# Moving the Gelu slope into the attention phase, and prefetching the gradient stage, in a fused transformer-block backward kernel

## The chip, the cores and the metric

The kernel runs on one core of one Trainium2 chip. The metric is the device time of one execution in microseconds. PE is the matmul engine, DVE the vector engine, ACT the activation engine, POOL the GpSimd engine, SP the engine that issues most transfers; 16 DMA engines move the data.

## The reference, cut to what matters

The program computes one block and all its gradients: `x + attention(xn) * silu(mlp(xn))`, S = 2048 rows, D = 512, 32 heads of 16, MLP width F = 1792, everything in bf16.

```python
x = A_x
xn = _layernorm(x)
s = _A_ref(xn, A_wqkv, A_wo)                 # softmax attention, 32 heads of 16
y = _layernorm(xn)
h = _gelu(y @ B_w1 + B_b1)                   # tanh form of Gelu
g = _silu(h @ B_w2 + B_b2)
out = x + s * g
# outputs: out, and the gradients of x, wqkv, wo, w1, b1, w2, b2 (jax.vjp)
```

The Gelu slope, gelu'(h1) with h1 = y·w1 + b1, is an F × S array (7.3 MB in bf16). It multiplies the incoming gradient in the MLP backward.

## The kernel before

It has three parts: a forward pre-stage (layer norms, qkv, MLP forward; it stores h1 in DRAM as `H1T_s`), attention forward and backward in one software-pipelined loop of 1024 steps, and a gradient stage for everything else.

One attention step, in program order (PE products `s`, `t`, `d`, exp on ACT, the product `gts` on DVE, then transposes by DMA from the SP queue):

```python
etp = sb("etp", 3); gtp = sb("gtp", 4); gbp = sb("gbp", 5); ekp = sb("ekp", 5)
...
for hj in range(2):    # emit_mult: one of these per head of the pair
    nc.vector.tensor_tensor(out=gts[:, kb % 2, hj, :]..., in0=ds[hj][:]..., in1=st_et[g][:, :, kb % 4, hj, :], op=ALU.mult)
# emit_dmat: every second step 512 KB of gts, every fourth step 512 KB of et, are transposed SBUF to SBUF
nc.sync.dma_start_transpose(out=blk[j]["Gk"][kc][:, h], in_=st_gt[g][:]...)          # gk <- gts
nc.sync.dma_start_transpose(out=ek[:]..., in_=st_et[g][:, 2:4]...)                   # ek <- et
```

The gradient stage computes the slope from h1 on ACT and DVE, in 28 groups of 1024 columns:

```python
def emit_gp(sc):                      # called four times, spread over the stage
    for f0, nf in FG:                 # 7 groups
        nc.scalar.dma_start(out=h1[:], in_=k.H1T_s[...])
        nc.scalar.activation(out=x2t[:], in_=h1[:], func=ACT.Square)
        ...                           # 7 DVE operations, 2 Sigmoids
```

Its order: output projection with `transpose_to` on PE for O and dm (`ps_so`), dwo, dw2, MLP gradient (`ps_dhg`, `ps_dy`), then one block of loads (wqkvT, dQT, R, xn, dQn, dKVn), dx and dwqkv (`ps_dxa`, `ps_dwq`), and dw1 (last group `ps_dw`).

Of the kernel before, what the change touches and what calls it, by code (L numbers as in the profile page):

```python
# [16 lines left out]
NT = S // 128  # L17
# [255 lines left out]
def phase3(ctx, tc, k, A_x, A_wqkv, A_wo, B_w1, B_w2, grad_out, out_0, out_1, out_2, out_3, out_4, out_5, out_6, out_7, dbg):  # L273
# [5 lines left out]
    GA = 0.044715  # L279
    GC = float(np.sqrt(2.0 / np.pi))  # L280
    FG = [(0, 2), (2, 2), (4, 2), (6, 2), (8, 2), (10, 2), (12, 2)]
    with ExitStack() as c1:
        big = c1.enter_context(tc.tile_pool(name="p3_big", bufs=1))
        psA = c1.enter_context(tc.tile_pool(name="p3_psA", bufs=5, space=PSUM))
        psT = c1.enter_context(tc.tile_pool(name="p3_psT", bufs=2, space=PSUM))
        psS = c1.enter_context(tc.tile_pool(name="p3_psS", bufs=1, space=PSUM))
        dxm_all = big.tile([128, NT, D], bf16, name="dxm_all")
        ones_bf = big.tile([128, 1], bf16, name="ones_bf")
        nc.vector.memset(ones_bf[:], 1.0)

        with ExitStack() as cAB:
            bAB = cAB.enter_context(tc.tile_pool(name="p3ab_big", bufs=1))
            gpp = cAB.enter_context(tc.tile_pool(name="p3_gp", bufs=3))
            gwk = cAB.enter_context(tc.tile_pool(name="p3_gwk", bufs=2))
            dmT = bAB.tile([128, IC, S], bf16, name="dmT")
            w2T = bAB.tile([128, IC, F], bf16, name="w2T")
            w1T = bAB.tile([128, FC, D], bf16, name="w1T")
            gps = {}
            dh_state = {}

            def emit_gp(sc):
                gp = gpp.tile([128, FC, 512], bf16, name="gp")
                gps[sc] = gp
                for f0, nf in FG:
                    h1 = gwk.tile([128, nf, 512], bf16, name="g_h1")
                    nc.scalar.dma_start(out=h1[:], in_=k.H1T_s[f0 * 128:(f0 + nf) * 128, sc * 512:(sc + 1) * 512].rearrange("(c p) s -> p c s", p=128))
                    x2t = gwk.tile([128, nf, 512], bf16, name="g_x2")
                    nc.scalar.activation(out=x2t[:], in_=h1[:], func=ACT.Square)
                    v = gwk.tile([128, nf, 512], bf16, name="g_v")
                    nc.vector.tensor_scalar(out=v[:], in0=x2t[:], scalar1=GA, scalar2=1.0, op0=ALU.mult, op1=ALU.add)  # L310
                    nc.vector.tensor_tensor(out=v[:], in0=v[:], in1=h1[:], op=ALU.mult)
                    sg = gwk.tile([128, nf, 512], bf16, name="g_sg")
                    nc.scalar.activation(out=sg[:], in_=v[:], func=ACT.Sigmoid, scale=2.0 * GC)
                    nc.vector.tensor_scalar(out=x2t[:], in0=x2t[:], scalar1=6.0 * GA * GC, scalar2=2.0 * GC, op0=ALU.mult, op1=ALU.add)
                    nc.vector.tensor_tensor(out=x2t[:], in0=x2t[:], in1=h1[:], op=ALU.mult)
                    nc.scalar.activation(out=v[:], in_=v[:], func=ACT.Sigmoid, scale=-2.0 * GC)
                    nc.vector.tensor_tensor(out=v[:], in0=v[:], in1=sg[:], op=ALU.mult)
                    nc.vector.tensor_tensor(out=v[:], in0=v[:], in1=x2t[:], op=ALU.mult)
                    nc.vector.tensor_tensor(out=gp[:, f0:f0 + nf, :], in0=v[:], in1=sg[:], op=ALU.add)

            with ExitStack() as c2:
                b2 = c2.enter_context(tc.tile_pool(name="p3a_big", bufs=1))
                wk = c2.enter_context(tc.tile_pool(name="p3a_wk", bufs=3))
                hgp = c2.enter_context(tc.tile_pool(name="p3a_hg", bufs=2))
                dm_all = b2.tile([128, NT, D], bf16, name="dm_all")
                otp = c2.enter_context(tc.tile_pool(name="p3a_ot", bufs=2))
                wo_sb = b2.tile([128, IC, D], bf16, name="wo_sb3")
                nc.sync.dma_start(out=wo_sb[:], in_=A_wo.rearrange("(c p) b -> p c b", p=128))
                hgcs = {}

                def load_hg(i):
                    hgcs[i] = hgp.tile([128, NT, 256], bf16, name="hgc")
                    nc.sync.dma_start_transpose(out=hgcs[i][:], in_=k.HGT_s[i * 256:(i + 1) * 256, :])
                psdb2 = psS.tile([1, D], f32, name="psdb2")
                for t in range(NT):
                    oT = otp.tile([128, IC, 128], bf16, name="oT")
                    transpose_to(nc, psT, oT, k.Oall[:, t, :], k.ident_bf, IC, 0, t)
                    ps = psA.tile([128, D], f32, name="ps_so", tag="mm")
                    for cc in range(IC):
                        nc.tensor.matmul(ps[:], lhsT=oT[:, cc, :], rhs=wo_sb[:, cc, :],  # L340
                                         start=(cc == 0), stop=(cc == IC - 1))
                    gb = wk.tile([128, 2, D], bf16, name="gb3")
                    (nc.sync if t % 2 == 0 else nc.scalar).dma_start(out=gb[:], in_=k.GB_s[t * 128:(t + 1) * 128, :, :])
                    xt = wk.tile([128, D], bf16, name="xt3")
                    (nc.scalar if t % 2 == 0 else nc.sync).dma_start(out=xt[:], in_=x2[t * 128:(t + 1) * 128, :])
                    nc.vector.tensor_tensor(out=dm_all[:, t, :], in0=ps[:], in1=gb[:, 1, :], op=ALU.mult)
                    t1 = wk.tile([128, D], f32, name="t13")
                    nc.vector.tensor_tensor(out=t1[:], in0=ps[:], in1=gb[:, 0, :], op=ALU.mult)
                    ot = wk.tile([128, D], bf16, name="ot3")
                    nc.gpsimd.tensor_tensor(out=ot[:], in0=t1[:], in1=xt[:], op=ALU.add)  # L350
                    nc.sync.dma_start(out=o0[t * 128:(t + 1) * 128, :], in_=ot[:])
                    transpose_to(nc, psT, dmT, dm_all[:, t, :], k.ident_bf, IC, t, 1)
                    nc.tensor.matmul(psdb2[0:1, :], lhsT=ones_bf[:, 0:1], rhs=dm_all[:, t, :], start=(t == 0), stop=(t == NT - 1))
                    if t == 1:
                        load_hg(0)
                    if t == 2:
                        load_hg(1)
                    if t == 3:
                        nc.sync.dma_start_transpose(out=w2T[:], in_=B_w2)
                        nc.sync.dma_start_transpose(out=w1T[:], in_=B_w1)  # L360
                db2 = wk.tile([1, D], bf16, name="db2")
                nc.vector.tensor_copy(out=db2[:], in_=psdb2[:])
                nc.sync.dma_start(out=out_7.rearrange("(o d) -> o d", o=1), in_=db2[:])
                emit_gp(0)
                dwo_ps = [psA.tile([128, D], f32, name="ps_dwo", tag="mm") for _ in range(IC)]
                for t4 in range(4):
                    dso = otp.tile([128, 4, D], bf16, name="dso3")
                    nc.scalar.dma_start(out=dso[:], in_=k.DSO_s[t4 * 512:(t4 + 1) * 512, :].rearrange("(t p) d -> p t d", p=128))
                    for ac in range(IC):
                        for tt in range(4):  # L370
                            t = t4 * 4 + tt
                            nc.tensor.matmul(dwo_ps[ac][:], lhsT=k.Oall[:, t, ac * 128:(ac + 1) * 128], rhs=dso[:, tt, :],
                                             start=(t == 0), stop=(t == NT - 1))
                for ac in range(IC):
                    dwo = otp.tile([128, D], bf16, name="dw_out")
                    nc.scalar.copy(out=dwo[:], in_=dwo_ps[ac][:])
                    nc.sync.dma_start(out=out_3[ac * 128:(ac + 1) * 128, :], in_=dwo[:])
                emit_gp(1)
                for i in range(7):
                    for fl in range(2):  # L380
                        fc = 2 * i + fl
                        ps = psA.tile([128, D], f32, name="ps_dw2", tag="mm")
                        for t in range(NT):
                            nc.tensor.matmul(ps[:], lhsT=hgcs[i][:, t, fl * 128:(fl + 1) * 128], rhs=dm_all[:, t, :], start=(t == 0), stop=(t == NT - 1))  # L384
                        dw2 = otp.tile([128, D], bf16, name="dw_out")
                        nc.scalar.copy(out=dw2[:], in_=ps[:])
                        nc.sync.dma_start(out=out_6[fc * 128:(fc + 1) * 128, :], in_=dw2[:])
                    if i + 2 < 7:
                        load_hg(i + 2)
# [526 lines left out]
```

## Time and profile before

The median is 2693.51 us in 3 runs (2687.11 to 2696.66); the profiled execution spans 2682.9 us.

| stretch, us of the span | length | what |
|---|---|---|
| 0–272 | 272 | pre-stage |
| 272–2191 | 1919 | attention |
| 2191–2683 | 492 | gradient stage |

Windows of the kernel before (start and end, length, then busy us of PE, its weight loads, DVE, ACT, POOL; granted PE clock; DMA share; GB/s). The DMA share adds up the times of all packets over the time of 16 engines, so it exceeds 1 where packets overlap. The rows are attention, projection, dw2, the block of loads, and dw1.

```profile
272.00:2191.00 1919.00, 1768.16 (x15620) 480.01 (x15620) 1548.33 (x2624) 1470.54 (x1537) 273.18 (x708) 0.99 1.15 228
2191.00:2291.00 100.00, 54.49 (x199) 18.43 (x200) 76.18 (x124) 52.85 (x62) 21.65 (x16) 0.51 0.77 195
2309.00:2364.00 55.00, 49.71 (x222) 21.64 (x220) 32.04 (x56) 33.20 (x41) 0.00 (x0) 0.97 0.87 180
2470.00:2526.00 56.00, 1.66 (x8) 0.58 (x6) 3.40 (x10) 2.20 (x4) 0.00 (x0) 0.56 1.06 259
2624.00:2683.00 59.00, 50.95 (x447) 44.00 (x445) 6.53 (x15) 5.22 (x14) 0.00 (x0) 0.97 0.56 123
```

In the projection PE runs at half clock with a chain of short dependences; in the 56 us hole PE does nothing. The hole, in the timeline of the SP queue (start, duration, line, what is issued):

```profile
2488.92 24.95 SPq L433 DMA_TRANSPOSE wqkvT<-in_A_wqkv_dram  x1
2513.92 9.72 SPq L434 DMA_TRANSPOSE dQT<-dQ_s  x1
2523.69 21.99 SPq L438 DMA_TRANSPOSE dKVn<-dKVT_s  x1
```

Last, gts, the DVE product on the chain of waits: its 2048 instances (min/median/max ns), and, from the view of waits in attention, how long DVE stood before it for a gts buffer that a gk transpose still held (us in total, times, longest).

```profile
L640 DVE TENSOR_TENSOR gts<-d,et x2048: 669/681/694, 286.5 to 2169.2; 128x512 bf16<-128x512 f32 x187
...
DVE gts L640 <- DMA gk<-gts: 0.8, 1, 0.8
```

### The profile page before, as it was taken

The page shows a single profiled execution, that of the slowest core. Times are in us where ns is not written, and L with a number is a line of the kernel's source. Part 1 is how long each engine was busy: PE and PEld are TensorE (multiplying, and loading weights), DVE is VectorE, ACT ScalarE, POOL GpSimd, SP SyncE. Part 2 cuts the span into 40 slices and gives each one's busy share as a digit, 9 for nine tenths or more (in the row PEclk, how much of TensorE's full clock was granted, in tenths as well). Part 3 has the DMA queues.
Part 4 walks back from the last instruction along what each step waited for, and adds up shares of the span by engine and source line. Part 5 has one row for each costly group of instructions (what it writes and reads, how often), then busy time and mean ns, then how long its engine had stood idle before and what let it go on. Part 6 is the DMA issues. An engine that isn't in the chain of part 4 may idle for free.

```text
span 2682.9 us, 47705 instructions
## 1 busy us (share of the span) xinstructions
PE 2317.8 (86%) x18320; PEld 743.1 (28%) x18320; DVE 1960.5 (73%) x3502; ACT 1733.7 (65%) x1951; POOL 404.5 (15%) x831
## 2 busy tenths in 40 slices
PE   3788799999999999999999999999999965888298
PEld 2333122222222222222222222222222212333147
DVE  5755688888888888888888888888888858775141
ACT  3344577777777777777777777777777755632020
POOL 0433202011110201111011111101111112000020
PEclk8899899999999999999999999999999975899699
DMA  5355999999999999999999999999999997634925
GB/s 188 94 183 179 190 243 225 227 235 230 229 230 237 222 233 227 228 232 232 232 222 236 227 233 232 227 234 225 231 229 235 217 216 187 157 93 97 309 70 116
DMA packets 1877879, 555.92 MB, mean 207 GB/s; under 512 B 1793553, under 2 KB 1861266, under 8 KB 1877650
## 3 DMA queue, kind: packets, MB, share of 16 engines
q1 hardware_dynamic: 1823874, 501.09, 91.9%
q10 hardware_dynamic: 53776, 51.78, 6.2%
q8 instruction: 143, 2.34, 0.4%
q14 instruction: 86, 0.70, 0.1%
HBM read 49.68 MB, written 57.41 MB: 40 GB/s over the span
## 4 chain that ended last, share of the span: by engine, by line
PE 37%; DVE 37%; issue 14%; DMA 7%; POOL 2%; ACT 1%; SPq 1%; ACTq 0%; DVEq 0%; POOLq 0%
DVE gts L640 29%; PE d L605 6%; PE X L686 6%; PE Z L755 4%; PE Z L749 3%; PE t L577 2%; DVE xs L692 2%; DVE xt L704 2%; PE ps_dhg L405 2%; PE ps_dwq L446 2%; PE XT L702 1%; PE X L671 1%; PE ps_h L212 1%; PE ps_dw L474 1%; PE ps_dw L384 1%
## 5 line engine op out<-in xcount | busy, mean ns | idle before, releaser
L640 DVE TENSOR_TENSOR gts<-d,et 128x512 bf16<-128x512 f32 x2048 | 1301.8, 682 | 324.2 <-issue 289.3
L619 ACT ACTIVATE et<-s 128x1024 bf16<-128x1024 f32 x1024 | 997.1, 1023 | 7.9 <-PE d L605 6.5
L627 ACT ACTIVATE e<-t 128x1024 bf16<-128x1024 f32 x512 | 524.3, 1024 | 424.9 <-PE t L577 421.3
L605 PE MATMUL d<-QDT,KVT 32*128 32x512 bf16 x2048 | 595.3, 378 | 117.7 <-DVE gts L640 116.5
L591 PE MATMUL s<-QDT,KVT 32*128 32x512 bf16 x2048 | 398.4, 386 | 14.8 <-DMA QDT<-QDPad 12.7
L671 PE MATMUL X<-et,Lc 128*32 128x512 bf16 x2048 | 398.0, 385 | 14.3 <-DVE xs L692 14.3
L674 PE MATMUL X<-et,NAT 128*32 128x512 bf16 x2048 | 399.1, 387 | 0.0
L686 PE MATMUL X<-gts,NAT 128*17 128x512 bf16 x2048 | 397.6, 384 | 0.0
L755 PE MATMUL Z<-gk,W 128*32 128x512 bf16 x2048 | 395.9, 380 | 0.0
L686 PEld LDWEIGHTS <-NAT 128*17 128x17 bf16 x2048 | 92.4, 87 | 492.1 <-issue 492.1
L719 POOL TENSOR_TENSOR W<-NATQd,rL 128x128 bf16<-128x128 bf16 x64 | 25.8, 403 | 1331.6 <-DVE rL L714 1331.6
L749 PE MATMUL Z<-e,W 128*32 128x512 bf16 x1024 | 201.0, 386 | 3.8 <-DVE acc L762 2.3
L749 PE MATMUL Z<-ek,W 128*32 128x512 bf16 x1024 | 201.8, 390 | 0.0
L577 PE MATMUL t<-KVT,QDT 32*128 32x512 bf16 x1024 | 199.5, 386 | 0.0
L591 PEld LDWEIGHTS <-KVT 32*128 32x128 bf16 x2048 | 96.6, 91 | 351.1 <-issue 351.1
L605 PEld LDWEIGHTS <-KVT 32*128 32x128 bf16 x2048 | 140.3, 90 | 69.2 <-issue 37.6
L671 PEld LDWEIGHTS <-Lc 128*32 128x32 bf16 x2048 | 103.6, 92 | 179.7 <-issue 179.7
L762 DVE TENSOR_TENSOR acc<-Z,acc 64x512 f32<-64x512 f32 x192 | 129.2, 673 | 13.3 <-PE Z L755 13.3
L749 PEld LDWEIGHTS <-W 128*32 128x32 bf16 x2048 | 120.9, 93 | 57.8 <-issue 51.3
L674 PEld LDWEIGHTS <-NAT 128*32 128x32 bf16 x2048 | 100.5, 95 | 50.6
L755 PEld LDWEIGHTS <-W 128*32 128x32 bf16 x2048 | 103.7, 95 | 8.2 <-issue 0.3
L577 PEld LDWEIGHTS <-QDT 32*128 32x128 bf16 x1024 | 48.2, 91 | 202.3 <-issue 202.3
(167 smaller groups left out, 2212.8 us busy)
## 6 DMA issues: line engine op xcount, KB each, us to landing
gk<-gts SPq DMA_TRANSPOSE x512, 4.2
HGT_s<-hgT SPq DMA_DIRECT2D x2, 3584.0 KB, 12.3
g_h<-H1T_s ACTq DMA_DIRECT2D x28, 256.0 KB, 3.3
DH1T_s<-dh1T SPq DMA_DIRECT2D x4, 1792.0 KB, 7.5
NAT<-NAT_s SPq DMA_DIRECT2D x16, 264.0 KB, 3.2
GB_s<-gB ACTq DMA_DIRECT2D x16, 256.0 KB, 2.0
ek<-et SPq DMA_TRANSPOSE x256, 4.1
dKVT_s<-ob SPq DMA_DIRECT2D x64, 64.0 KB, 2.2
```

The source lines that it names most:

```text
L577: nc.tensor.matmul(t[:, hj, :], lhsT=op["QDT"][r:r + 32, q0:q0 + 128], rhs=op["KVT"][r:r + 32, kc * 512:(kc + 1) * 512], start=True, stop= ...
L591: nc.tensor.matmul(s[:, hj, :], lhsT=op["KVT"][r:r + 32, kb * 128:(kb + 1) * 128], rhs=op["QDT"][r:r + 32, qc * 512:(qc + 1) * 512], start ...
L605: nc.tensor.matmul(d[:], lhsT=op["KVT"][r:r + 32, kb * 128:(kb + 1) * 128], rhs=op["QDT"][r:r + 32, qc * 512:(qc + 1) * 512], start=True, ...
L619: nc.scalar.activation(out=et[:, :, kb % 4, :, :].rearrange("k b h q -> k h b q"), in_=st_s.pop(g)[:].rearrange("k h (b q) -> k h b q", b= ...
L627: nc.scalar.activation(out=e[:], in_=st_t.pop(g)[:], func=ACT.Exp)
L640: nc.vector.tensor_tensor(out=gts[:, kb % 2, hj, :].rearrange("k (b q) -> k b q", b=4), in0=ds[hj][:].rearrange("k (b q) -> k b q", b=4), ...
L671: nc.tensor.matmul(X[64 + 32 * hj:96 + 32 * hj, :], lhsT=Lc[:], rhs=et[:, :, kb % 4, hj, :], start=(kb == 0), stop=False, skip_group_check ...
L674: nc.tensor.matmul(X[32 * hj:32 * hj + 32, :], lhsT=NATt[:, kb, hj, 1:33], rhs=et[:, :, kb % 4, hj, :], start=(kb == 0), stop=(kb == 15), ...
L686: nc.tensor.matmul(X[64 + 32 * hj:64 + 32 * hj + 17, :], lhsT=NATt[:, kb, hj, 0:17], rhs=gts[:, kb % 2, hj, :], start=False, stop=(kb == 1 ...
L749: nc.tensor.matmul(Z[32 * hj:32 * hj + 32, :], lhsT=blk[j]["W1"][:, qb, hj, :], rhs=ev[:, hj], start=(qb == qb_order[0]), stop=False, tile ...
L755: nc.tensor.matmul(Z[32 * hj:32 * hj + 32, :], lhsT=blk[j]["W2"][:, qb, hj, :], rhs=gv[:, :, :, hj, qb, :], start=False, stop=(qb == qb_or ...
L762: nc.vector.tensor_tensor(out=av, in0=Z[0:64, :], in1=av, op=ALU.add)
```

## The change

Its intent: the slope is made on POOL during attention, where POOL is idle 86% of the time, a tile of 128 × 512 at a time, one POOL operation per attention step; the result goes to DRAM (`GP_s`) and the gradient stage only loads it. That frees DVE, ACT and SBUF in the gradient stage, which is rewritten: PE transposes become DMA transposes, operands are loaded early into slots shared by tag, dwq is interleaved with the projection and dkv follows it, gradients are computed one group ahead.

The core of the diff (long parts cut):

```diff
 # attention: a generator that is advanced by one operation per step
+    def gelu_slope_ops():
+        def load(i):
+            x = bgp.tile([128, 512], bf16, name="bg_x")
+            nc.sync.dma_start(out=x[:], in_=H1T_s[fc * 128:(fc + 1) * 128, sc * 512:(sc + 1) * 512])
+        for i in range(4 * FC):                       # 56 tiles
+            tt(m, x, x);  yield
+            ts(v, m, GA, 1.0);  yield
+            tt(v, v, x);  yield
+            nc.scalar.activation(out=t[:], in_=v[:], func=ACT.Tanh, scale=GC)
+            ts(m, m, 1.5 * GA * GC, 0.5 * GC);  yield
+            tt(m, m, x);  nx = load(i + 1);  yield
+            ...                                       # five more POOL operations
+            nc.sync.dma_start(out=GP_s[fc * 128:(fc + 1) * 128, sc * 512:(sc + 1) * 512], in_=m[:])
+            yield
...
             emit_finalize((g - 17) // 16)
+        elif g % 16 not in (2, 3):
+            next(bg, None)
 # gradient stage
-            def emit_gp(sc):                          # slope on ACT and DVE: gone
+        def load_gp(i):
+            gps[i] = ring.tile([128, 7, 512], bf16, name="gp", bufs=3)
+            nc.scalar.dma_start(out=gps[i][:], in_=k.GP_s[...])
...
-                    transpose_to(nc, psT, oT, k.Oall[:, t, :], k.ident_bf, IC, 0, t)
+                nc.sync.dma_start_transpose(out=oT[i][:]..., in_=k.Oall[:, 4 * i:4 * i + 4, :]...)
...
+                for ic in range(IC):                  # dwq beside the projection
+                    nc.tensor.matmul(acc4[ic][:], lhsT=xn_all[:, t, ic * 128:(ic + 1) * 128], rhs=k.dQall[:, t, :], ...)
...
-            nc.sync.dma_start_transpose(out=wT[:], in_=A_wqkv)
-            nc.sync.dma_start_transpose(out=dQT[:], in_=k.dQ_s)
-            nc.sync.dma_start_transpose(out=dKVn[:], in_=k.dKVT_s)
+            do_D(3)
+            load_hg(k.DH1T_s, 0)
+            wT = big.tile([128, 12, D], bf16, name="wqkvT", tag="s14a")
+            nc.sync.dma_start_transpose(out=wT[:], in_=A_wqkv)
```

## The prediction

> **What bounds the kernel now.** The stage windows split the 2682.9 us span into: forward pre-stage 0–272, attention 272–2191 (1919 us), gradient stage 2191–2683 (492 us). In attention PE is busy 1768, DVE 1548, ACT 1471, POOL 273 us; the chain of waits alternates between the DVE product gts (29% of the span), PE matmuls and PE issue. No engine has room for more, except POOL. In the gradient stage PE is busy only 365 of 492 us. Its matmuls are about 1440 of 512 columns (the dw1 ones counted as halves); at the 0.216 us each that the dhg run shows (56 in 12.1 us) that is 311 us, so 181 us are waits, a cold clock, and transposes on PE. The windows say where: output projection 2191–2291, 100 us at a granted clock of 0.5, for a cadence of 5 us per row tile in its quiet half; operand loads 2470–2526, 56 us with PE idle (the queue view shows the issues of wqkvT 25, dQT 9.7 and dKVn 22 us in a row on SP); dw2 55 us and dw1 59 us against 48 us of matmuls each, waiting for 1 MB transposes that land in 7–8.5 us.
>
> **What the change does.**
> 1. Removes from the gradient stage the slope chain: 28 groups of about 4.3 us of DVE (119 us) and 3.1 us of ACT.
> 2. PE transposes of O and dm become DMA transposes, so the projection loses its PE–copy–PE round trip; dwqkv (192 matmuls, 41 us) moves there.
> 3. Operands are loaded ahead: the 56 us hole should nearly vanish.
> 4. Adds to attention 56 × (nine or ten POOL operations, one Tanh, two 128 KB transfers).
>
> **Costing the attention part.** Like POOL operations take 0.65–1.5 us (q 0.82–1.23, ot 1.45), about 10 us per tile, 560 us in all; POOL goes from 273 to about 830 of 1919 us and stays off the chain. The Trainium skill's page "SBUF — State Buffer", section "Who interferes with whom", says that a DVE instruction with at most one SBUF input outside the two-port modes does not contend with GpSimd. gts, acc, xs and xt are such, and the trace agrees so far: gts takes 669 to 694 ns in all 2048 cases, POOL running or not. "ScalarE: Activation LUTs", section "Table sets", puts tanh in the set of exp, so no table reloads; no trace here shows it yet. Tanh costs about 0.6 us (estimate from 1.02 us for 1024 columns); ACT has 0.6–0.7 us idle before each e, so about half is hidden: +20 us (0 to +50).
>
> **Costing the gradient stage.** The projection becomes bound by transfers and SP issue: roughly 24 MB at the 290 GB/s that transposes reach is 83 us, so it ends near +84 instead of +100, with a third of dwqkv inside. Then dkv 28, db2 and dwo 18, dw2 53, D/E 100, dx 48, dw1 52, tail 3: about 386 us, saving 106.
>
> **Prediction.** 2693.5 − 106 + 20 ≈ 2607 us, range 2550 to 2665. Faster by over 2%: 0.80; within 2%: 0.17; slower: 0.03.
>
> **What would show it.** gts still 0.68 us; no table loads in attention; attention 1920–1970 us; POOL near 45% there; no PE hole before ps_dxa; projection window 70–95 us, with SP busy issuing transposes throughout; PE busy in the gradient stage near 330 us.
>
> **What would make it wrong.** Tanh reloading tables, or POOL locking DVE or delaying W1/W2 (attention +100 us or more); SP issue of the new stores stuck behind POOL and delaying gk; transposes crowding the projection beyond 110 us, or wT landing late before dx. On the good side: a warm clock and faster transposes could make the gradient stage 350 us.

## More of the kernel before

From the page of the kernel before: busy time of each engine, then DMA business in tenths and the rate moved, each in 40 slices of the span, then the HBM part.

```profile
PE 2317.8 (86%) x18320; PEld 743.1 (28%) x18320; DVE 1960.5 (73%) x3502; ACT 1733.7 (65%) x1951; POOL 404.5 (15%) x831
...
DMA  5355999999999999999999999999999997634925
GB/s 188 94 183 179 190 243 225 227 235 230 229 230 237 222 233 227 228 232 232 232 222 236 227 233 232 227 234 225 231 229 235 217 216 187 157 93 97 309 70 116
...
HBM read 49.68 MB, written 57.41 MB: 40 GB/s over the span
```

POOL looks free. But in attention (slices 5 to 32) the DMA row stands at 9 and the rate is flat at about 230 GB/s, while HBM averages only 40 GB/s over the span: nearly all of it is the transposes, which stay inside SBUF.

## The result, and the profile after

The median is 2632.47 us (2626.5 to 2635.03, 4 runs) against 2693.29 us (2687.11 to 2696.66, 4 runs). The ratio is 0.9774, 95% interval 0.9749 to 0.9798: 2.3% faster. (Ratios are the mean time of one kernel's fast runs over the mean of the other's fast runs of the same rounds, so they are not quite the ratio of the medians quoted.) The gain is 61 us where 86 was predicted.

The page of the kernel after:

```profile
PE 2295.2 (87%) x18152; PEld 731.6 (28%) x18192; DVE 1837.6 (70%) x3286; ACT 1673.4 (64%) x1910; POOL 908.0 (35%) x1391
...
DMA  5355899999999999999999999999999998987475
GB/s 192 92 184 184 179 239 232 236 236 234 226 236 237 237 231 237 231 234 242 231 235 233 237 228 240 235 236 233 226 233 229 236 218 183 271 215 186 153 160 125
...
HBM read 52.83 MB, written 62.66 MB: 44 GB/s over the span
```

While the slope is made (slices 4 to 25) the rate is a little higher, about 235 GB/s, and the DMA row as full as ever. Windows of the kernel after: attention; then the gradient stage: wait for the first operands, projection with dwq, dkv, dw2, MLP gradient, dw1.

```profile
271.00:2223.00 1952.00, 1785.37 (x15616) 479.72 (x15616) 1549.00 (x2624) 1501.26 (x1593) 781.48 (x1267) 0.98 1.16 231
...
2223.00:2244.00 21.00, 0.58 (x1) 0.29 (x3) 0.66 (x1) 0.00 (x0) 0.61 (x1) 0.58 1.07 303
2244.00:2306.00 62.00, 36.47 (x126) 14.32 (x127) 17.95 (x29) 1.07 (x2) 13.75 (x12) 0.80 1.17 260
2306.00:2354.00 48.00, 36.24 (x143) 14.98 (x145) 3.26 (x5) 5.27 (x9) 4.61 (x4) 0.80 0.96 231
2368.00:2418.00 50.00, 48.02 (x218) 21.45 (x222) 0.00 (x0) 8.19 (x14) 0.00 (x0) 1.00 0.76 186
2418.00:2515.00 97.00, 96.63 (x444) 43.98 (x450) 63.49 (x189) 22.98 (x46) 0.00 (x0) 1.00 0.67 170
2562.00:2625.00 63.00, 50.32 (x437) 43.23 (x434) 14.35 (x34) 10.30 (x24) 5.33 (x5) 0.92 0.56 127
```

So attention went from 1919 to 1952 us (+33), and the gradient stage from 492 to 402 us (−90). The hole before dx is gone (SP now issues wqkvT while PE is busy with the MLP gradient). The first 131 us of the gradient stage (to 2354) moved 303 × 21 + 260 × 62 + 231 × 48 GB/s·us = 33.6 MB, 256 GB/s on average.

gts in the kernel after, and the wait in front of it; then, from the groups of ACT in attention, the Tanh and the only table load:

```profile
L743 DVE TENSOR_TENSOR gts<-d,et x2048: 669/681/693, 284.9 to 2204.0; 128x512 bf16<-128x512 f32 x187
...
DVE gts L743 <- DMA gk<-gts: 30.2, 17, 3.9
```

```profile
L638 ACT ACTIVATE bg_t<-bg_v 128x512 f32<-128x512 f32 x56 | 35.5, 635 | 4.8 <-POOL bg_v L631 4.8
L722 ACT ACT_TABLE_LOAD x1 | 1.3, 1283 | 14.5 <-PE d L708 14.5
```

gts itself is not a nanosecond slower with POOL busy. What is new is that DVE stands 30 us waiting for gts buffers whose transpose is late. Taking the start of the first product of each step (of 1024) from both traces, attention's length from first to last gts is 1882 us before and 1918 us after. The mean step is 1.888 us up to step 758, in which the slope is made, against 1.839 us before; after step 758 it is 1.840 against 1.841 us. The whole loss (36 us by this measure) thus lies in the steps with slope work.

Within these steps the loss is not spread evenly. Cut both traces into the 47 cycles of 16 steps that hold slope work, and set each cycle beside the same one before: 29 cycles have lost less than 0.25 us, the other 18 carry the whole loss. The DMA engines move 234 GB/s in the first and 233 in the second, but 431 KB a step in the first and 457 KB in the second. It reads like a backlog that most cycles push ahead and some pay for. Seven of the 18, with 26 us of the loss, also hold stretches of 3.4 to 13.7 us in which PE is granted half its clock (eight stretches, 41 us in all; one of 3.4 us before). Each begins 0.8 to 3.2 us after a gts that had waited 1.4 to 3.9 us, so the waits come first. How much the slower PE then adds to the loss no run separates.

At the end of attention, in the chain of waits of the gradient stage (start, length, what):

```profile
2222.79 7.10 DMA oT<-Oall
2229.90 4.53 DMA dKVT_s<-ob
2234.90 8.51 DMA gb<-GB_s
...
2268.70 11.72 DMA gb<-GB_s
```

### The profile page after: what moved, and what is told of

The parts are those of the page before. It is cut to its first block, busy times and chain, and to the rows that moved or that the text cites. A ratio compares the mean times of both kernels' runs of the same rounds, so it can differ in the third digit from the quotient of the medians.

```text
span 2624.7 us, 47762 instructions
## 1 busy us (share of the span) xinstructions
PE 2295.2 (87%) x18152; PEld 731.6 (28%) x18192; DVE 1837.6 (70%) x3286; ACT 1673.4 (64%) x1910; POOL 908.0 (35%) x1391
## 4 chain that ended last, share of the span: by engine, by line
PE 38%; DVE 33%; issue 12%; DMA 10%; ACT 4%; POOL 2%; SPq 0%; ACTq 0%; DVEq 0%; POOLq 0%
DVE gts L743 26%; PE d L708 6%; PE X L789 6%; PE Z L858 4%; DMA gk<-gts 4%; PE Z L852 3%; PE t L680 3%; PE X L774 2%; PE ps_dhg L463 2%; DVE xs L795 2%; ACT et L722 2%; DVE xt L807 2%; PE XT L805 1%; PE ps_dw L528 1%; PE ps_dw L442 1%
## 5 line engine op out<-in xcount | busy, mean ns | idle before, releaser
L722 ACT ACTIVATE et<-s 128x1024 bf16<-128x1024 f32 x1024 | 1002.6, 1024 | 24.9 <-PE d L708 13.8
L774 PE MATMUL X<-et,Lc 128*32 128x512 bf16 x2048 | 403.9, 391 | 14.1 <-DVE xs L795 14.1
L852 PEld LDWEIGHTS <-W 128*32 128x32 bf16 x2048 | 121.1, 93 | 56.7 <-issue 50.2
L631 POOL TENSOR_TENSOR bg_v<-bg_t 128x512 f32<-128x512 f32 x56 | 58.1, 1038 | 149.1 <-ACT bg_t L638 149.1
L870 POOL CAST ob<-acc 64x512 bf16<-64x512 f32 x64 | 38.6, 603 | 203.3 <-DVE acc L865 203.3
```

The costliest lines, as they stand in the source:

```text
L722: nc.scalar.activation(out=et[:, :, kb % 4, :, :].rearrange("k b h q -> k h b q"), in_=st_s.pop(g)[:].rearrange("k h (b q) -> k h b q", b= ...
L774: nc.tensor.matmul(X[64 + 32 * hj:96 + 32 * hj, :], lhsT=Lc[:], rhs=et[:, :, kb % 4, hj, :], start=(kb == 0), stop=False, skip_group_check ...
L852: nc.tensor.matmul(Z[32 * hj:32 * hj + 32, :], lhsT=blk[j]["W1"][:, qb, hj, :], rhs=ev[:, hj], start=(qb == qb_order[0]), stop=False, tile ...
```

## The experiments

Two questions: why attention lost 36 us rather than 20, and where the gradient stage kept 16 us more than the 386 predicted. For attention there are four theories: **ACT** (the Tanh delays exp; it was in the prediction), **POOL** (its work delays W1 and W2, two operands that POOL makes for the Z products, or slows other engines), **SP** (112 more issues on a queue that is nearly always issuing), and **bytes** (14.7 MB more on the DMA engines). Adding up the issues on SP over the 758 steps, it is issuing 92% of the time before and 94% after, and the median lag from a finished gts pair to the issue of its transpose grows from 2.5 to 4.1 us. That made SP the favourite.

All results, with "attention" from the first to the last gts product, "wait" the DVE idle time before gts put down to gk transposes, and "rest" the time from the last gts to the end:

| run | median us | ratio to before (95%) | attention | wait | rest |
|---|---|---|---|---|---|
| before | 2693 | 1 | 1882 | 1 | 514 |
| after | 2632 | 0.9774 (0.9749–0.9798) | 1918 | 30 | 421 |
| p1_slope_only | 2727 | 1.0152 (1.0123–1.0181) | 1917 | 22 | 513 |
| p2_no_slope | 2595 | 0.9654 (0.9630–0.9678) | 1880 | 3 | 428 |
| e1_actq | 2630 | 0.9775 (0.9751–0.9799) | 1915 | 25 | 421 |
| e2_no_tanh | 2640 | 0.9814 (0.9791–0.9837) | 1924 | 33 | 423 |
| e3_gts5 | 2634 | 0.9785 (0.9759–0.9811) | 1920 | 1 | 420 |
| e4_no_dma | 2600 | 0.9664 (0.9634–0.9693) | 1884 | 2 | 428 |
| e5_dma_only | 2641 | 0.9818 (0.9789–0.9846) | 1930 | 39 | 424 |
| e6_double | 2697 | 1.0022 (0.9994–1.0050) | 1979 | 85 | 422 |
| g1_dqt_late | 2634 | 0.9790 (0.9767–0.9813) | 1923 | 37 | 421 |
| g2_dw1_ahead | 2623 | 0.9743 (0.9722–0.9765) | 1928 | 29 | 410 |
| g3_order | 2633 | 0.9776 (0.9754–0.9798) | 1927 | 35 | 420 |
| b3_split | 2606 | 0.9694 (0.9671–0.9717) | 1908 | 12 | 410 |

after, p1, g1, g2 and g3 have the same attention; its length varies from 1917 to 1928 us from one profile to another. Attention therefore lost 35 to 46 us, and differences of 10 us between single profiles mean nothing.

### p1_slope_only and p2_no_slope: the two halves of the change apart

```diff
 # p1: the kernel before, with the slope generator of the kernel after in attention; GP_s is not used
+        elif g % 16 not in (2, 3):
+            next(bg, None)
 # p2: the kernel after, without it; the gradient stage loads h1 instead
-        elif g % 16 not in (2, 3):
-            next(bg, None)
-            nc.scalar.dma_start(out=gps[i][:], in_=k.GP_s[...])
+            nc.scalar.dma_start(out=gps[i][:], in_=k.H1T_s[...])
```

> The kernel before plus only the slope made in attention (computed and stored, its result not used; outputs right). If the attention loss is the slope's alone, attention (first to last gts) goes from 1882 to about 1918 us as in the kernel after, the gradient stage stays near 492, and the time is about 2693 + 36 = 2729 us. If the loss came from something else in the new layout (places of Oall and dQall), it stays near 2693.

> The kernel after without the slope in attention; the gradient stage reads h1 in its place (so two of the outputs are wrong on purpose, work and bytes of the gradient stage the same). Expected: attention back to 1882 us from first to last gts, gradient stage still near 402 us, time about 2632 - 36 = 2596 us. If the two halves of the change interfere, the gradient stage differs from 402.

Both came out as expected: 2727 and 2595 us. The slope costs 1.5% by itself, the new gradient stage saves 3.5% by itself, and 1.0152 × 0.9654 = 0.980 is close to the 0.977 of both. So the loss belongs to the slope in attention and not to the new layout. (p2's two wrong outputs are those of w1 and b1, on purpose.)

### e1_actq: the slope's transfers issued from ACT

```diff
-            nc.sync.dma_start(out=x[:], in_=H1T_s[...])
+            nc.scalar.dma_start(out=x[:], in_=H1T_s[...])
...
-            nc.sync.dma_start(out=GP_s[...], in_=m[:])
+            nc.scalar.dma_start(out=GP_s[...], in_=m[:])
```

> The kernel after, with the slope's 56 loads and 56 stores issued from the ACT queue instead of SP; same bytes, same POOL and Tanh work. Theory SP (the SP queue, 91% busy issuing in attention before and 95% with the slope, issues gk transposes later, so gts waits for its buffers): the lag from gts to the gk issue falls back from a median of 4.1 to about 2.5 us, gts waits for DMA gk fall from 30 us to near 0, attention loses only 5 to 15 us instead of 36, time about 2605 to 2615 us. Theory ACT (the Tanh delays exp): no gain, 2632 or more, as ACT has the issues on top. Theory DMA (the bytes themselves crowd the transposes): no gain.

Theory SP falls: 2630 us, no gain, and gts still waits 25 us for gk. The 112 issues had taken SP 63 us; with them gone SP is as occupied as before (94% of the time in the slope's steps), because the mean issue of a transpose grew from 2.13 to 2.22 us. That fits an issue whose length is set by how fast the DMA engines take the work, and not by the cost of issuing; no run shows this directly. The median time from issue to landing of gk stays at 4.2 us before, 4.1 after and 4.4 here: what grows is the lag before the issue. On issuing engines the Trainium skill, "DMA: Bandwidth & Descriptors", section "Issuing engines are not separate DMA queues", says that transfers started by different engines run on the same 16 DMA engines and that a second issuing engine saves only the issue time. This run agrees, at 0.9775 against 0.9774.

### e2_no_tanh: no Tanh on ACT

```diff
-            nc.scalar.activation(out=t[:], in_=v[:], func=ACT.Tanh, scale=GC)
-            tt(v, t, t)
-            ts(v, v, -1.0, 1.0)
+            tt(t, v, v)
+            ts(v, t, -1.0, 1.0)
```

> The kernel after without the Tanh on ACT (POOL uses v where the tanh stood; gradient outputs wrong on purpose; POOL operations and transfers unchanged). Theory ACT: attention back to about 1885 to 1890 us from first to last gts, time about 2600. Theory SP: gts waits for DMA gk stay near 30 us, attention stays within 8 us of 1918, time 2622 to 2632.

Theory ACT falls too: attention 1924 us, in the spread of the kernel after. The time of 2640 us is above the 2622 to 2632 expected; the intervals of the ratios (0.9814 against 0.9774) just overlap, and the difference stays unexplained.

### e4_no_dma and e5_dma_only: the work without the bytes, the bytes without the work

```diff
 # e4: POOL and Tanh stay; one load in all, no store (the gradient stage loads h1)
-            if i + 1 < 4 * FC:
-                nx = load(i + 1)
-            nc.sync.dma_start(out=GP_s[...], in_=m[:])
 # e5: all loads and stores in their places, no POOL operation, no Tanh
-            tt(m, x, x)
-            ...
-            nc.sync.dma_start(out=GP_s[...], in_=m[:])
+            nc.sync.dma_start(out=GP_s[...], in_=x[:])
```

> The kernel after with all POOL operations and the Tanh of the slope kept, but only its first load and none of its stores (the gradient stage reads h1 instead; two outputs wrong on purpose). The queue and the Tanh having fallen as sole causes, theory bytes says: the slope's 14.7 MB compete on the 16 DMA engines with the transposes, which run at 230 GB/s already, so without them attention falls from 1918 to 1880 to 1890 us from first to last gts, gts waits for DMA gk near 0, time 2595 to 2605 us. Theory POOL (the POOL work delays W1, W2 or slows other engines): attention stays above 1905 us, time above 2620.

> The kernel after with the slope's loads and stores at the same places on the same queue, but no POOL operation and no Tanh (h1 itself is stored; two outputs wrong on purpose). Theory bytes: attention stays at 1905 to 1920 us, gts waits for DMA gk 20 us or more, time 2620 to 2632. Theory POOL: attention near 1882, time near 2595.

These two decide it. With all the POOL and ACT work and no bytes, attention is 1884 us: nothing lost. With the bytes alone it is 1930 us: everything lost, even 10 us more than the range expected (2641 us in all where 2620 to 2632 was said). The waits of DVE before gts, in e4 and then in e5:

```profile
DVE gts L740 <- DMA gk<-gts: 2.1, 2, 1.3
```

```profile
DVE gts L721 <- DMA gk<-gts: 39.2, 20, 3.7
```

The window 300–1700 us of e4 and of e5 (columns as before):

```profile
300.00:1700.00 1400.00, 1299.23 (x11530) 353.11 (x11530) 1145.29 (x1941) 1113.72 (x1191) 701.29 (x1071) 1.00 1.17 231
```

```profile
300.00:1700.00 1400.00, 1279.19 (x11176) 343.75 (x11171) 1109.60 (x1881) 1055.81 (x1102) 194.47 (x506) 0.98 1.17 233
```

So the 500 us of POOL work and the 35 us of Tanh that the change put into attention are nearly free (2600 us against the 2595 of p2, intervals overlapping), and what costs is the transport to and from POOL's tiles. The granted clock goes with the bytes too and not with POOL's work: it is at half for 0 us of the slope's steps in p2, 7 in e4, 58 in e5.

### e6_double: the dose

```diff
             nc.sync.dma_start(out=x[:], in_=H1T_s[...])
+            nc.sync.dma_start(out=y[:], in_=H1T_s[...])
...
             nc.sync.dma_start(out=GP_s[...], in_=m[:])
+            nc.sync.dma_start(out=GP2_s[...], in_=m[:])
```

> The kernel after with every load and every store of the slope made twice (29.4 MB instead of 14.7 MB in attention; POOL and ACT work unchanged; outputs right). Theory bytes, attention at the ceiling of the DMA engines: the rate stays at 232 to 238 GB/s and the time grows with the bytes, by 40 to 65 us more, attention about 1960 to 1980 us from first to last gts, time 2675 to 2695. If the engines still had room and only bursts cost, the second copy adds less than 25 us.

Attention is 1979 us, 2697 us in all (2 us above the range expected): the second 14.7 MB eat the whole gain of the change. The window 300–1700 us (columns as before; the last is GB/s) of the kernel before, of the kernel after and of e6:

```profile
300.00:1700.00 1400.00, 1301.71 (x11539) 353.83 (x11538) 1146.27 (x1943) 1087.35 (x1138) 197.53 (x515) 1.00 1.17 231
```

```profile
300.00:1700.00 1400.00, 1285.61 (x11264) 345.25 (x11258) 1119.46 (x1896) 1090.29 (x1165) 692.14 (x1055) 0.98 1.18 235
```

```profile
300.00:1700.00 1400.00, 1259.86 (x10799) 332.67 (x10796) 1075.85 (x1819) 1049.30 (x1117) 663.04 (x1007) 0.95 1.16 235
```

Twice the extra bytes, and the rate stays at 235 GB/s: that is the ceiling for this mix. The kernel before ran at 231, 2% below it. (e5, which lost as much, ran at 233, so the ceiling is good to about 1%.) PE is at half clock for 143 us of the slope's steps, against 41 in the kernel after. The count closes, as an estimate that checks the bytes, since the rates are measured in the same runs: before, a step of 1.839 us at 231 GB/s moves 425 KB; the slope adds 14.7 MB / 758 = 19.4 KB a step, and 444 KB at 235 GB/s take 1.890 us (measured 1.888); doubled, 464 KB take 1.973 us (measured 1.968). These are means over quiet and losing cycles. e6 doubles the number of transfers along with the bytes, so whether the cost goes by bytes or by transfers is not separated.

### e3_gts5: one more buffer

```diff
-    gtp = sb("gtp", 4)
+    gtp = sb("gtp", 5)
-            v = bgp.tile([128, 512], f32, name="bg_v", bufs=1)      # t likewise
+            v = bgp.tile([128, 512], bf16, name="bg_v", bufs=1)
```

> The kernel after with 5 instead of 4 gts buffers (v and t of the slope in bf16 to make room; outputs within tolerance). If the loss is made of late landings that the four buffers can't hide, one more buffer (two steps, 3.7 us of slack) takes gts waits for DMA gk from 30 us to under 8, and attention to 1890 to 1900 us, time about 2610. If the DMA engines are simply full, the wait only moves elsewhere and the time stays within 6 us of 2632.

The wait moved and the time stayed, at 2634 us. Waits before gts in e3 (ACT is named for the et buffers, which in turn wait for the other transpose, ek; in the kernel after these two waits are 29.5 and 7.0 us):

```profile
DVE gts L743 <- ACT et L722: 53.5, 32, 14.2
...
ACT et L722 <- DMA ek<-et: 38.8, 25, 3.6
...
DVE gts L743 <- DMA gk<-gts: 0.9, 1, 0.9
```

Here one more buffer in front of the full resource cured nothing.

### g1_dqt_late: an early load put late

```diff
             load_oT(3)
-            for i in range(4):
-                nc.sync.dma_start_transpose(out=dQT[:, 4 * i:4 * i + 4]..., in_=k.dQall[...]...)
...                                                       # behind the dw2 loop
+            for i in range(4):
+                nc.sync.dma_start_transpose(out=dQT[:, 4 * i:4 * i + 4]..., in_=k.dQall[...]...)
+            dxm_all = k.pO.tile([128, NT, D], bf16, name="dxm_all", tag="slotB")
```

> The kernel after with the four dQT transposes (16 us of SP issue at the start of the gradient stage, used only 250 us later) moved behind the dw2 loop, where the DMA engines have room. If the projection is bound by what SP and the DMA engines must bring first, dwo starts 12 to 16 us earlier (131 us after attention now) and the time is about 2618 us. If it is bound by the gb and xt loads of the ACT queue, less than 5 us are gained.

No gain: dwo starts 127 us after attention instead of 131, 2634 us in all. The timeline of SP in this run shows why it was a poor test: the gradient stage is not issued in written order but in the order of the framework's scheduler, which filled the gap with hg and w2T (both needed much later) and issued dQT still before dwo.

```profile
2252.57 6.86 SPq L301 DMA_TRANSPOSE hgc<-HGT_s  x1
2259.53 11.81 SPq L384 DMA_TRANSPOSE w2T<-in_B_w_dram  x1
...
2339.62 13.23 SPq L445 DMA_TRANSPOSE dQT<-dQall  x4
```

### g3_order: written order, loads by need

```diff
+            with tc.manual_schedule():
+                phase3(ctx, tc, k, ...)
...                                  # inside: gb(0), a quarter of xn, gb(1) first; then as needed
-                if t == 9:
-                    nc.sync.dma_start_transpose(out=w2T[:], in_=B_w2)
-                if t == 13:
-                    nc.sync.dma_start_transpose(out=w1T[:], in_=B_w1)
...                                  # w2T in the dkv stage, w1T and dQT behind dw2
```

> The kernel after with the gradient stage issued in written order instead of the scheduler's, and the loads written by need: first gb, the first quarter of xn and O, later the rest; slope halves after dwo (the scheduler drew the first two, 1.8 MB, ahead of the first operands), w2T in the dkv stage, w1T and dQT behind dw2. Theory transfers (33.6 MB in the 131 us before dwo, at 257 GB/s): some 6.5 MB fewer there, the first projection matmul 12 us after attention instead of 20, dwo starts at 105 to 115 us, time 2610 to 2620 us. If written order loses overlap elsewhere, the time is above 2632.

The first half of the expectation holds: the first projection matmul comes 11 us after attention instead of 20, dwo starts at 111 instead of 131 us. The projection takes all of that gain (60 us from the end of attention to the first dkv matmul instead of 83); dkv takes 51 us instead of 48. But the time is 2633 us: what was gained before dwo was given back. dw2 and dw1 of g3, in windows:

```profile
2354.00:2414.00 60.00, 50.84 (x223) 22.40 (x227) 0.00 (x0) 8.88 (x16) 0.00 (x0) 0.94 0.94 236
...
2558.00:2632.00 74.00, 53.55 (x455) 44.79 (x453) 20.96 (x50) 16.20 (x36) 10.13 (x8) 0.95 0.49 120
```

dw2 takes 60 us instead of 50, now itself at 236 GB/s with the bytes that were put off, and at a granted clock of 0.94; dw1 takes 69 instead of 61 us in written order. The stretch before dwo moved 248 × 60 + 244 × 51 GB/s·us = 27.3 MB instead of 33.6 MB. With the chain of waits above, which is mostly DMA there, this points to the transfers as what sets the pace of the projection; but the run changes the order of the instructions as well, so it does not prove it. It does not give a better kernel.

### g2_dw1_ahead: dw1 fed earlier

In the kernel after, the view of waits for 2562–2625 us shows PE and its weight loads standing for chunks of dh1:

```profile
PEld L528 <- DMA hgc<-DH1T_s: 9.5, 3, 8.6
...
PE ps_dw L528 <- DMA hgc<-DH1T_s: 8.7, 2, 8.4
```

```diff
+            hg2 = c2.enter_context(tc.tile_pool(name="p3c_hg", bufs=2))    # two more chunks on chip
+            def load_hg2(i): ...
...                                                    # in the dx loop, ahead of the dx stores
+                if t in (2, 7):
+                    load_hg2(2 if t == 2 else 3)
```

> The kernel after with four instead of two transposed chunks of dh1 on chip for dw1, chunks 2 and 3 asked for during the dx stage ahead of the dx stores on the SP queue. dw1 takes 61 us now, 48 of them matmuls; PE stands at two chunks for about 12 us. If the late chunks are the cause, dw1 takes 50 to 53 us and the time falls by 8 to 11 us, to about 2622. If the transposes of 1 MB can't run faster than 7.4 us each, the gain is below 4 us.

dw1 takes 54 us instead of 61, "rest" falls from 421 to 410 us, the time is 2623 us. The intervals of the ratios (0.9743 against 0.9774) overlap a little, so the timing alone would not prove it; the profile shows the waits gone from dw1.

### b3_split: the slope where there is room

If bytes are what attention lacks, part of the slope should be made elsewhere. In the gradient stage DVE is busy 3 us in the 112 us of dkv, dwo and dw2. The kernel loads three of the eight slope parts there anyway; loading h1 in their place costs the same bytes and spares attention 21 of 56 tiles.

```diff
 # on top of g2_dw1_ahead
-        nx = load(0)
+        nx = load(21)                                  # attention makes tiles 21 to 55 only
...
-            nc.scalar.dma_start(out=gps[i][:], in_=k.GP_s[...])
+            nc.scalar.dma_start(out=gps[i][:], in_=(k.H1T_s if i < 3 else k.GP_s)[...])
...
+            def slope_here(n):                         # 12 groups, in place, temporaries in slots
+                nc.scalar.activation(out=x2, in_=h, func=ACT.Square)     # that the projection has left
+                ts(v, x2, GA, 1.0)
+                tt(v, v, h)
+                nc.scalar.activation(out=th, in_=v, func=ACT.Tanh, scale=GC)
+                ...                                    # six more on DVE
+                tt(h, x2, th, ALU.add)
```

> The kernel with dw1 fetched ahead, and the slope split by where there is room: its first three eighths (21 of 56 tiles) are made in the gradient stage by DVE and ACT, which stand idle during dwqkv, dwo and dw2 (DVE about 3 us busy in the 112 us before the MLP gradient), in place of loading the ready slope, so that attention moves 9.2 MB instead of 14.7. Theory bytes: attention loses 20 to 30 us instead of 36 to 45, the gradient stage stays at 390 to 395 us, time about 2623 - 14 = 2609 us (2600 to 2616). If the DVE chain comes late for the MLP gradient, the gain is eaten there: PE waits for gp, time 2620 or more.

It came out at 2606 us (2604 to 2614, 5 runs), ratio 0.9694: 3.1% faster than the kernel before and 0.8% faster than the kernel after (0.9694 / 0.9774 = 0.992), with correct outputs. Part of that is dw1 fed earlier: against g2, on which it is built, the split alone gives 0.5% (0.9694 / 0.9743 = 0.995). Attention is 1908 us, the rest is 410 us as in g2, and the wait before gts is down:

```profile
DVE gts L776 <- DMA gk<-gts: 12.0, 8, 2.6
```

## Why the prediction was right or wrong

The measured 2632 us lie inside the range of 2550 to 2665, and the call "faster by over 2%" held. The gain of 61 us is 25 less than the 86 predicted. Point by point:

- *"gts still 0.68 us; no table loads in attention"*: right. gts takes 669 to 693 ns beside 500 us more of POOL work, as the Trainium skill's "SBUF — State Buffer", section "Who interferes with whom", has it for instructions with one SBUF input; and one table load stands in attention, for exp and tanh together, as "ScalarE: Activation LUTs", section "Table sets", has it.
- *"POOL stays off the chain"*: right, and e4 shows that the whole of POOL and ACT work costs nearly nothing (2600 us against 2595). The window has POOL at 781 of 1952 us, 40%, near the 45% said.
- *"+20 us"* for attention: the step that failed. It was charged to the Tanh on ACT, which e2 and e4 show to cost nothing that can be measured. The true term, the two 128 KB transfers per tile, was listed under point 4 and then not costed. It measured 35 to 46 us. That the loss stayed in the range of 0 to +50 is luck: the range was meant for another cause. Behind it is the sentence *"No engine has room for more, except POOL"*, which counted compute engines and left out the 16 DMA engines. The page had a hint, though no proof: DMA at 9 in every slice of attention. (The flat rate of 230 GB/s would also fit the steady demand of a loop; e6 shows that it was close to the ceiling.) The 290 GB/s that the prediction used as the rate of transposes was a peak of short stretches; the sustained ceiling in attention is about 235.
- *"SP issue of the new stores stuck behind POOL and delaying gk"*, among the things that could go wrong: the symptom (late gk) came, the cause was another one: e1 took those issues away without gain.
- *The hole before dx vanishes; projection window 70 to 95 us; PE busy near 330 us*: right. It is 83 us (2223 to 2306) and 328 us.
- *"about 386 us"* for the gradient stage: 402 measured. The last matmul of the projection came 5 us earlier than said (at 79 us, and the first of dkv at 83), dw2, the MLP gradient and dx were together 8 us shorter, dw1 9 us longer (g2 points to the two late chunks), and dkv with db2 and dwo took 66 us instead of 46. That last term was taken as PE-bound at full clock. In the 48 us window of dkv PE is busy only 36 us, and at a granted clock of 0.80; its 128 matmuls at 0.216 us would be 28. The projection was costed about right (22.5 MB at 271 GB/s against 24 MB at 290); not costed were the 11.1 MB that moved during dkv. The scheduler also drew slope parts, needed only 170 to 196 us later, to the start of the stage. How much of the 20 us is waiting for transfers, how much the lower clock, and what better order could save is not settled: g3 brought dwo 20 us earlier, but in the projection and not in dkv, and lost the time again later.

The two misses add up: about 13 us in attention (33 instead of 20 by the window) and 16 in the gradient stage, less about 4 us: the profiled spans differ by 58 us where the medians differ by 61, and the pre-stage is 1 us shorter.

## What to carry to other kernels

Before moving work to an idle engine, cost the transport of its operands on the resource that is fullest in that stretch, and count the DMA engines as one: a busy share of 9 with a flat rate over the whole stage says that they may be at their ceiling, whatever the HBM rate is, and a run with extra bytes tells (e6). To tell a busy issue queue from full DMA engines, move the issues to another queue, and to tell the work from the bytes, run each without the other. When a stage has several resources near full, split the work so that each part goes where its scarce resource is free: here five eighths in attention and three eighths in the gradient stage beat all of it in attention (0.9694 against the 0.9743 of g2). All of it in the new gradient stage was not tried.

## What the Trainium skill lacked or had wrong

- "Perfetto Trace Analysis", section "What "DMA-bound" means", reads an issuing track that is solid with DMA slices as descriptor generation. Here SP was issuing 92 to 94% of the time, and taking 112 issues away only lengthened the mean issue of a transpose from 2.13 to 2.22 us, with no gain in time (ratio 0.9775 against 0.9774): DMA engines at their ceiling can look the same on that track.
- The same page, section "Identifying the Most-Contended Engine", takes HBM utilization as the measure for DMA, by which the page means all DMA traffic over a peak of 358 GB/s per core. For this attention loop that makes 231 / 358 = 65%, and yet the engines gave no more than 235 GB/s when twice the extra bytes were asked for (e6). Taken as HBM traffic alone it says even less: 40 GB/s over the span.
- "DMA: Bandwidth & Descriptors", section "Latency and other measured facts", gives DMA transposes an effective 261 GB/s, or 350 to 400 when contiguous. In this kernel's attention, where most of the traffic is SBUF-to-SBUF transposes of 512 KB with few plain transfers between them, all traffic together ran at 231 to 235 GB/s and at no more when more was asked (e6).
